# Attention and mixture of experts on one core: three sums put behind the next block's sixth product, and loads moved at the pass edges

## The chip, the cores and the metric

The kernel runs on 1 core of one Trainium2 chip. The metric is the device time of one execution in microseconds (us). Engines are named as in the profile: PE is TensorE, DVE is VectorE, ACT is ScalarE, POOL is GpSimd, SP is SyncE, which here issues all DMAs in one queue (SPq).

## What is computed

```python
def _attn_ref(q, k, v):                      # q, k, v: (4, 8, 576, 64)
    scores = scale * np.matmul(q, k.transpose(0, 1, 3, 2))
    mask = (rel >= 0) & (rel < 64)           # rel = query position - key position
    scores = np.where(mask, scores, -1e9)
    ...
    return np.matmul(softmax(scores), v)

def _moe_ref(x, w_gate, w1, w2):             # x: (2304, 512), E = 8, F = 1024
    P = np.exp(logits - logits.max())        # logits = x @ w_gate
    for _ in range(8):
        P /= P.sum(1, keepdims=True) + 1e-9
        P /= P.sum(0, keepdims=True) + 1e-9
        P *= N / E
    for e in range(E):
        out += P[:, e:e + 1] * (np.maximum(x @ w1[e], 0.0) @ w2[e])
```

All of it is float32. A matrix product is made of three products of rounded parts (high by high, high by low, low by high), so each operand is kept as a high part and a low part.

## The kernel before

The 2304 rows of x are 18 tiles of 128. A first stage computes attention and the gate (to about 207 us of the span). Then the experts run in three passes over six tiles each: pass 0 (to about 682 us), pass 1 (to about 1150 to 1182 us) and pass 2. The hidden columns of all experts form 30 groups of 256 columns; two groups make a unit, so there are 15 units (the first half of expert 0 was done in the first stage).

**First products (x by w1).** A group is computed as 2x2 blocks in Winograd's form: seven block products in the order 1, 5, 6, 2, 7, 3, 4 (`Group.product`, L212, six matmuls of 128x384 each) that add up in three PSUM tiles qa, qb, qc of two buffers each. ACT copies intermediate values (`b` from `a`, `p5`, `u2`), DVE makes the sums.

**Pass 0** (`Group.run`, then `mm2`): per unit two groups and then six ordinary second products (L271). While it runs, POOL and ACT split the weights into high and low parts, and these go to DRAM: w1 to `w1d`, and four sums of w2's blocks (`sums2`, four DVE operations per group, run one at a time by `sum_step`, L184) to `w2d`. The Sinkhorn iteration (`sk_col`, `sk_row`, L733 to L743) is spread over the second products of the first units by `step()`. `fetch2` loads raw w2 into one of four `stg` buffers.

**Passes 1 and 2.** Both products are in Winograd's form. `First(p, i)` (F_i below) is the first product of group i, `Second(p, u, o)` (S_u.o) one third of the second product of unit u; a number behind it is the block product, as in F2.4 or S0.0.7. The order of blocks is F0, F1, F2, S0.0, S0.1, S0.2, F3, F4, S1.0 and so on (`plan`), and within a block 6, 2, product 1 of the next block, 7, 3, product 5 of the next block, 4. The order is written out by hand: each engine runs its instructions in the order in which the code emits them. A `Second` product is six matmuls of 128x256 (L975); DVE adds its result to `acc` (`out_add`, L981), and the next product into the same PSUM tile waits for that.

After product 4 of a First block, DVE runs four operations in a row: sm0 (`relu_op`, L949) of qb, sm1 of c22 and sm0, sm3 of qc and sm1, and the low part `lo(1)` of qc (L900). POOL makes sm2 from sm1 and r22 (L954). The four results sm0 to sm3 are then split (`part_s`: ACT L903, POOL L904); the first at once, three by way of the list `urgent`. `bulk` is a list of w2 blocks to split (`split_w2`: ACT L882, POOL L883, then the next load `wr` by `load_w2`, L877, of three buffers). `do_bulk(1)` takes one entry, from `urgent` first.

**Pass edges.** Hooks behind given products load w1 of a later group (`load_w1`, L699, four DMAs into one of two `w1c` buffers, after product 4 of the group two before), store the finished rows (`out_rows`, L1031), reload the accumulator with the first stage's part for the new rows (`acc_rows`, L1035, six DMAs) and scale it (`scale0`, L1038, six DVE operations).

Of the kernel before, what the change touches and what calls it, by code (L numbers as in the profile page):

```python
# [11 lines left out]
ALU = mybir.AluOpType  # L12
# [9 lines left out]
def window_attention_sinkhorn_moe(ctx: ExitStack, tc: tile.TileContext, q, k, v, w_gate, w1, w2, out):  # L22
    nc = tc.nc
# [294 lines left out]
    with tc.manual_schedule():  # L318
# [383 lines left out]
        with ExitStack() as p2:  # L702
# [63 lines left out]
            for u in range(n_units):  # L766
                s = 2 * u
                last = u == n_units - 1

                def even(k):  # L770
                    if k == 0 and u > 0:
                        sum_step()
                        keep2(s + 2)
                    if k == 1:
                        if u:
                            split2(s + 2)
                            fetch1(s + 3)
                        keep1(s + 1 if u else 0)
                    elif k == 3:
                        if 4 <= u < 7:  # L780
                            next_sums(2, u - 4)
                        elif u == 7:
                            nc.sync.dma_start(out=xd_t[2], in_=side["xt"])
                        elif 9 <= u < 12:
                            next_sums(1, u - 9)

                def odd(k):
                    if k == 0 and u > 0:
                        sum_step()
                    if u == 0:  # L790
                        if k == 1:
                            split2(1)
                            fetch1(2)
                            keep1(1)
                    elif k == 0:
                        sums1(s + 2)
                    elif k == 1:
                        split2(s + 3)
                        fetch2(s + 4)
                        keep2(s + 3)  # L800

                Group(s).run(even)
                if last:
                    load_w1(0)
                Group(s + 1).run(odd)
                if last:
                    load_x(1, (0, 1, 2))
                    load_w1(1)
                if u == 0:
                    split2(2)  # L810
                    fetch1(3)
                    sums1(2)
                    split1(2)
                    split2(3)
                    fetch2(4)
                else:
                    split1(s + 2)
                sums1(s + 3)
                fetch2(s + 5)
                if last:  # L820
                    for k in (3, 4, 5, 6):
                        high_x(k)
                for t in range(TP):
                    if t == 0:
                        sums2(s + 4)
                        sums2(s + 5)
                    mm2(u, t)
                    sum_step(2 if last and t > 3 else 1)
                    if t % 2 == 0:
                        step()  # L830
                    if t == 2:
                        split1(s + 3)
                        fetch1(s + 4)
                    if t == 3 and not last:
                        keep1(s + 2)
                    if last:
                        low_x((3, 4, 5, 6, None, None)[t]) if t < 4 else None
                        if t == 4:
                            keep2(s + 4)
                if last:  # L840
                    keep2(s + 5)
# [3 lines left out]
        with ExitStack() as p3:  # L845
# [7 lines left out]

            HD = 2 * P
            W, R, G7 = {}, {}, {}
            bulk, urgent = [], []
            done_s = set()

            def do_bulk(n):
# [27 lines left out]
            def queue_w2(pu, ks):  # L887
                if pu:
                    bulk.extend([lambda k=k: split_w2(*pu, ORDER[k]) for k in ks])

            class First:
                def __init__(self, p, i):
                    self.p, self.i, self.G = p, i, Group(i)
# [13 lines left out]
                def step(self, n):  # L907
                    G = self.G
                    if n == 1:
                        self.a, self.b = ps["a"](), ps["b"]()  # L910
                        G.product(1, self.a, True)
                        nc.scalar.copy(out=self.b, in_=self.a)
                        do_bulk(1)
                    elif n == 5:
                        self.c, self.p5 = ps["c"](), new("p5", [P, NB], F32, 1)
                        G.product(5, self.c, True)
                        nc.scalar.copy(out=self.p5, in_=self.c)
                        do_bulk(1)
                    elif n == 6:
                        self.u2 = new("u2", [P, NB], F32, 1)  # L920
                        G.product(6, self.b, False)
                        nc.scalar.copy(out=self.u2, in_=self.b)  # L922
                        do_bulk(1)
                    elif n == 2:
                        self.g = new("G", [P, 7, 2, NB], F32R, 3)
                        G7[self.p, self.i] = self.g
                        self.r22 = new("r22", [P, NB], F32, 1)
                        G.product(2, self.a, False)
                        nc.scalar.activation(out=self.r22, in_=self.a, func=AF.Relu)
                        self.hi(2, self.a)  # L930
                    elif n == 7:
                        self.c22 = new("c22", [P, NB], F32, 1)
                        G.product(7, self.b, False)
                        G.add(self.c22, self.b, self.p5)
                        self.hi(0, self.c22)
                        self.lo(2, self.a)
                    elif n == 3:
                        G.product(3, self.c, False)
                        G.add(self.c, self.c, self.u2)
                        self.hi(1, self.c)  # L940
                        self.lo(0, self.c22)
                    else:
                        while urgent:
                            urgent.pop(0)()
                        G.product(4, self.b, False)
                        sm = self.sm = [new(f"sm{k}", [P, NB], F32, 1) for k in range(4)]

                        def relu_op(dst, src, other, op):
                            nc.vector.scalar_tensor_tensor(out=dst, in0=src, scalar=0.0, in1=other, op0=ALU.max, op1=op)  # L949

                        relu_op(sm[0], self.b, self.r22, ALU.add)
                        relu_op(sm[1], self.c22, sm[0], ALU.subtract)
                        relu_op(sm[3], self.c, sm[1], ALU.add)
                        nc.gpsimd.tensor_tensor(out=sm[2], in0=sm[1], in1=self.r22, op=ALU.add)  # L954
                        self.lo(1, self.c)
                        self.part_s(0)
                        urgent.extend([lambda k=k: self.part_s(k) for k in (1, 2, 3)])
                        wt1.pop(self.i)

            class Second:  # L960
                def __init__(self, p, u, o):
# [4 lines left out]
                def product(self, n, bank, start):  # L966
                    gp, wp = PROD[n]
                    p, u = self.p, self.u
                    while (p, u, wp) not in W or (p, 2 * u + 1, gp) not in done_s:
                        do_bulk(1)  # L970
                    cols = slice(self.o * P, (self.o + 1) * P)
                    j = 0
# [10 lines left out]
                def step(self, n):  # L983
# [10 lines left out]
                    elif n == 6:  # L994
                        self.product(6, self.b, False)
                        self.out_add(1, 1, self.b)
                    elif n == 2:
                        self.product(2, self.a, False)
                        self.out_add(1, 0, self.a)
# [47 lines left out]

            for _ in range(3):
                load_w2()
            queue_w2((1, 0), range(7))  # L1050
            out_rows(0, range(TP))
            first = plans[0][1][0]
            first.step(1)
# [2 lines left out]
            for p, F, S, flow in plans:  # L1056
# [5 lines left out]
                def hook(blk, step, *fs):  # L1062
                    hooks.setdefault((blk, step), []).extend(fs)

                hook(F[0], 6, lambda p=p: acc_rows(p))
                for i in range(n):
                    if i + 2 < n:
                        hook(F[i], 4, lambda i=i: load_w1(i + 2))
                    elif more:
                        hook(F[i], 4, lambda i=i: load_w1(i + 2 - n))  # L1070
                for t, (i, st) in enumerate(((1, 6), (1, 2), (1, 4), (2, 6), (2, 2), (2, 7))):
                    hook(F[i], st, lambda p=p, t=t: scale0(p, t))
                last = S[-1]
                if more:
                    hook(F[n - 1], 2, lambda p=p: new_x(p + 1))
# [11 lines left out]
                for k, blk in enumerate(flow):  # L1087
                    nx = flow[k + 1] if k + 1 < len(flow) else None
                    for st in (6, 2, -1, 7, 3, -5, 4):
                        if st > 0:  # L1090
                            go(blk, st)
                        elif nx:
                            go(nx, -st)
                a, b, c = last
                for blk, st in ((a, 1), (b, 1), (a, 2), (b, 2), (a, 5), (b, 5), (a, 6), (b, 6), (a, 7), (b, 7), (a, 3), (b, 3), (a, 4), (c, 1), (b, 4), (c, 5), (c, 6), (c, 2), (nextF, 1), (c, 7), (c, 3), (nextF, 5), (c, 4)):
                    if blk:
# [31 lines left out]
```

## Time and profile before

| | |
|---|---|
| median of 3 runs | 1646.04 us (1645.75 to 1646.67) |
| the profiled execution | 1643.92 us, span 1642.1 us, mean granted PE clock 0.992 |
| PE busy | 1580.5 us (96%), weight loads 1494.1 us |
| DVE, ACT, POOL busy | 912.2, 768.1, 973.8 us |
| chain that ended last | PE 84%, DVE 8% (3% at L949), DMA 4% |

The profile has a start time, a duration and the idle time before for each instruction. A row of the timeline reads: start in us, duration in us, engine, line, operation, output tile <- input tiles, shapes, how many instructions the row merges, and in square brackets the idle time of the engine just before and what ended it. Matmul ends are modelled with the pipeline's tail (a row of six matmuls lasts about 0.16 us longer than the distance to the next row), so idle time of PE is shown somewhat too small.

### The profile page before, as it was taken

The page shows a single profiled execution, that of the slowest core. Times are in us where ns is not written, and L with a number is a line of the kernel's source. Part 1 is how long each engine was busy: PE and PEld are TensorE (multiplying, and loading weights), DVE is VectorE, ACT ScalarE, POOL GpSimd, SP SyncE. Part 2 cuts the span into 40 slices and gives each one's busy share as a digit, 9 for nine tenths or more (in the row PEclk, how much of TensorE's full clock was granted, in tenths as well). Part 3 has the DMA queues.
Part 4 walks back from the last instruction along what each step waited for, and adds up shares of the span by engine and source line. Part 5 has one row for each costly group of instructions (what it writes and reads, how often), then busy time and mean ns, then how long its engine had stood idle before and what let it go on. Part 6 is the DMA issues. An engine that isn't in the chain of part 4 may idle for free.

```text
span 1642.1 us, 29136 instructions
## 1 busy us (share of the span) xinstructions
PE 1580.5 (96%) x10875; PEld 1494.1 (91%) x10875; DVE 912.2 (56%) x1754; ACT 768.1 (47%) x1676; POOL 973.8 (59%) x912
## 2 busy tenths in 40 slices
PE   8999989999999999979999999999899999999998
PEld 7888879989989989879999999999799999999998
DVE  6666456565555555454554554555565455455455
ACT  6566534433433433334544544544444454454452
POOL 5244466677776875165565565565566556556554
PEclk9999999999999999989999999999999999999999
DMA  9876476567667565854555555555855555555551
GB/s 223 193 162 151 140 247 240 205 225 273 233 236 256 212 237 212 291 211 165 184 184 171 183 186 172 182 187 170 309 181 185 171 184 185 172 182 186 172 181 65
DMA packets 206974, 324.50 MB, mean 198 GB/s; under 512 B 68528, under 2 KB 137136, under 8 KB 202864
## 3 DMA queue, kind: packets, MB, share of 16 engines
q1 hardware_dynamic: 206832, 322.64, 60.0%
q8 instruction: 85, 1.39, 0.3%
q14 instruction: 57, 0.47, 0.1%
HBM read 227.56 MB, written 88.08 MB: 192 GB/s over the span
## 4 chain that ended last, share of the span: by engine, by line
PE 84%; DVE 8%; DMA 4%; POOL 1%; ACT 1%; issue 1%; SPq 0%; DVEq 0%; POOLq 0%; ACTq 0%
PE qb L212 16%; PE yp L271 13%; PE qa L212 11%; PE qc L212 11%; PE qb L975 11%; PE qc L975 8%; PE qa L975 5%; DVE sm L949 3%; PE yp L556 3%; PE hp L542 3%; PE vp L462 1%; DMA stg<-in_moe_w_dram 1%; DVE G L900 1%; PE sp L412 1%; DMA wr<-w2d 1%
## 5 line engine op out<-in xcount | busy, mean ns | idle before, releaser
L883 POOL TENSOR_TENSOR wp<-wr,wp 128x512 fp32r<-128x512 f32 x210 | 270.3, 1305 | 178.5 <-ACT wp L882 174.5
L212 PE MATMUL qb<-xc,w1c 128*128 128x384 f32 x1620 | 323.0, 337 | 5.2 <-ACT u L922 4.8
L212 PEld LDWEIGHTS qb<-xc,w1c 128*128 128x128 f32 x1620 | 282.5, 189 | 6.2 <-ACT u L922 5.4
L904 POOL TENSOR_TENSOR G<-sm,G 128x384 fp32r<-128x384 f32 x240 | 241.1, 1032 | 47.8 <-ACT G L903 47.8
L975 PE MATMUL qb<-wp,G 128*128 128x256 f32 x1620 | 232.5, 286 | 24.8 <-DVE acc L981 24.8
L271 PE MATMUL yp<-w2c,g 128*128 128x512 f32 x1080 | 252.1, 392 | 0.6 <-DVE acc L290 0.6
L975 PEld LDWEIGHTS qb<-wp,G 128*128 128x128 f32 x1620 | 214.6, 191 | 30.9 <-DVE acc L981 30.7
L271 PEld LDWEIGHTS yp<-w2c,g 128*128 128x128 f32 x1080 | 202.9, 189 | 42.9 <-DVE acc L290 1.1
L212 PE MATMUL qa<-xc,w1c 128*128 128x384 f32 x1080 | 215.3, 339 | 10.6 <-DMA w1c<-w1d 10.6
L981 DVE SCALAR_TENSOR_TENSOR acc<-qb,prob,acc 128x256 f32<-128x256 f32 x270 | 130.3, 483 | 152.7 <-PE qb L975 152.5
L212 PE MATMUL qc<-xc,w1c 128*128 128x384 f32 x1080 | 214.4, 338 | 0.0
L212 PEld LDWEIGHTS qa<-xc,w1c 128*128 128x128 f32 x1080 | 190.6, 190 | 12.3 <-issue 11.1
L212 PEld LDWEIGHTS qc<-xc,w1c 128*128 128x128 f32 x1080 | 190.8, 190 | 0.0
L954 POOL TENSOR_TENSOR sm<-sm,r 128x384 f32<-128x384 f32 x60 | 61.1, 1018 | 184.4 <-DVE sm L949 156.2
L975 PE MATMUL qc<-wp,G 128*128 128x256 f32 x1080 | 150.2, 284 | 3.3 <-POOL wp L883 3.2
L903 ACT CAST G<-sm 128x384 fp32r<-128x384 f32 x240 | 120.6, 514 | 66.8 <-DVE sm L949 61.0
L173 POOL TENSOR_TENSOR w2c<-stg,w2c 128x512 fp32r<-128x512 f32 x60 | 83.6, 1415 | 112.1 <-PE qb L212 99.6
L975 PE MATMUL qa<-wp,G 128*128 128x256 f32 x1080 | 149.4, 283 | 0.5
L882 ACT CAST wp<-wr 128x512 fp32r<-128x512 f32 x210 | 124.6, 622 | 46.0 <-DMA wr<-in_moe_w_dram 36.6
L975 PEld LDWEIGHTS qc<-wp,G 128*128 128x128 f32 x1080 | 140.4, 193 | 3.7 <-POOL wp L883 3.4
L975 PEld LDWEIGHTS qa<-wp,G 128*128 128x128 f32 x1080 | 139.6, 191 | 1.3 <-DVE G L900 0.7
L225 DVE TENSOR_TENSOR c<-qb,p 128x384 f32<-128x384 f32 x60 | 33.4, 557 | 170.9 <-PE qb L212 169.0
(160 smaller groups left out, 2129.5 us busy)
## 6 DMA issues: line engine op xcount, KB each, us to landing
w1c<-w1d SPq DMA_DIRECT2D x180, 512.0 KB, 5.5
w1d<-w1c SPq DMA_DIRECT2D x30, 1792.0 KB, 7.0
stg<-in_moe_w_dram SPq DMA_DIRECT2D x66, 512.0 KB, 4.1
wr<-w2d SPq DMA_DIRECT2D x120, 256.0 KB, 3.1
wr<-in_moe_w_dram SPq DMA_DIRECT2D x90, 256.0 KB, 2.8
w2d<-tf SPq DMA_DIRECT2D x30, 512.0 KB, 3.6
w1c<-w1d SPq DMA_DIRECT2D x60, 256.0 KB, 2.8
xd_r<-xs SPq DMA_DIRECT2D x36, 128.0 KB, 2.7
```

What stands on the lines that cost most here:

```text
L173: nc.gpsimd.tensor_tensor(out=w[:, 1], in0=src[:, j], in1=f32(w[:, 0]), op=ALU.subtract)
L212: nc.tensor.matmul(bank, lhsT=w[:, ws, a, kk, :], rhs=xc[xs][:, b, kk, :], start=(first and j == 0), stop=(j == 5), skip_group_check=not f ...
L271: nc.tensor.matmul(yp, lhsT=g[:, a, o:o + P], rhs=w[:, x, :], start=(i == 0), stop=(i == 11))
L542: nc.tensor.matmul(hp, lhsT=w1s[c][:, a, kk, :], rhs=xs[j][:, b, kk, :], start=(i == 0), stop=(i == 3 * KD - 1))
L556: nc.tensor.matmul(yp, lhsT=g[:, a, o * P:(o + 1) * P], rhs=w[:, x, :], start=(i == 0), stop=(i == 11))
L882: nc.scalar.copy(out=t[:, :, 0, :], in_=r)
L883: nc.gpsimd.tensor_tensor(out=t[:, :, 1, :], in0=r, in1=f32(t[:, :, 0, :]), op=ALU.subtract)
L903: nc.scalar.copy(out=self.g[:, 3 + k, 0, :], in_=self.sm[k])
L904: nc.gpsimd.tensor_tensor(out=self.g[:, 3 + k, 1, :], in0=self.sm[k], in1=f32(self.g[:, 3 + k, 0, :]), op=ALU.subtract)
L954: nc.gpsimd.tensor_tensor(out=sm[2], in0=sm[1], in1=self.r22, op=ALU.add)
L975: nc.tensor.matmul(bank, lhsT=G7[p, 2 * u + g][:, gp, x, cols], rhs=W[p, u, wp][:, g, y, :], start=(start and j == 0), stop=(j == 5), skip ...
L981: nc.vector.scalar_tensor_tensor(out=at, in0=src, scalar=prob[:, FIRST[self.p] + t, self.e:self.e + 1], in1=at, op0=ALU.mult, op1=ALU.add)
```

## The change

Four things move; no operation is added or taken away.

1. In `First.step(4)` only sm0 and the split of sm0 are left. sm1, sm3, sm2, `lo(1)` and the entries for `urgent` go into a list `after`, which `late_sums()` runs in step 6 of the next block: behind the ACT copy in a First block, behind `out_add` in a Second block (and where the list is needed earlier, and after the last block of the flow).
2. In pass 0 the steps of `sums2` are dealt out otherwise: none behind the first two second products of unit 0, three in the even group and one in the odd group of a unit. The last two raw w2 groups are fetched about a unit earlier.
3. The w2 blocks of pass 1's first unit are put on the list `bulk` after F0.2 and not before F0.1; `do_bulk(1)` is also called after products 7 and 3 of the first three groups of pass 1.
4. The accumulator's reload goes from F0.6 to F1.6, its scaling from F1 and F2 to F2.3 (two operations) and products 2 and 3 of S0.0 and S0.1.

```diff
@@ pass 0
 def even(k):
+    if k != 1:
+        sum_step()
     if k == 0 and u > 0:
-        sum_step()
         keep2(s + 2)
     if k == 1:
...
+        if last:
+            fetch2(s + 5)
...
 def odd(k):
-    if k == 0 and u > 0:
+    if k == 0:
         sum_step()
...
-        fetch2(s + 4)
+        if not last:
+            fetch2(s + 4)
...
-fetch2(s + 5)
+if not last:
+    fetch2(s + 5)
...
     mm2(u, t)
-    sum_step(2 if last and t > 3 else 1)
+    if u or t > 1:
+        sum_step(2 if last and t > 3 else 1)
...
     if t == 2:
         split1(s + 3)
         fetch1(s + 4)
+        if u == n_units - 2:
+            fetch2(s + 6)
@@ passes 1 and 2
+def late_sums():
+    while after:
+        after.pop(0)()
...
     elif n == 6:                                     # First
         nc.scalar.copy(out=self.u2, in_=self.b)
+        late_sums()
         do_bulk(1)
...
     elif n == 7: ...                                 # First, and the same in n == 3
+        if self.p == 1 and self.i < 3:
+            do_bulk(1)
...
     relu_op(sm[0], self.b, self.r22, ALU.add)        # First, n == 4
-    relu_op(sm[1], self.c22, sm[0], ALU.subtract)
-    relu_op(sm[3], self.c, sm[1], ALU.add)
-    nc.gpsimd.tensor_tensor(out=sm[2], in0=sm[1], in1=self.r22, op=ALU.add)
-    self.lo(1, self.c)
     self.part_s(0)
-    urgent.extend([lambda k=k: self.part_s(k) for k in (1, 2, 3)])
     wt1.pop(self.i)
+
+    def rest():
+        relu_op(sm[1], self.c22, sm[0], ALU.subtract)
+        relu_op(sm[3], self.c, sm[1], ALU.add)
+        nc.gpsimd.tensor_tensor(out=sm[2], in0=sm[1], in1=self.r22, op=ALU.add)
+        self.lo(1, self.c)
+        urgent.extend([lambda k=k: self.part_s(k) for k in (1, 2, 3)])
+
+    after.append(rest)
...
     elif n == 6:                                     # Second
         self.product(6, self.b, False)
         self.out_add(1, 1, self.b)
+        late_sums()
...
-queue_w2((1, 0), range(7))
...
-hook(F[0], 6, lambda p=p: acc_rows(p))
+if p == 1:
+    hook(F[0], 2, lambda: queue_w2((1, 0), range(7)))
...
-for t, (i, st) in enumerate(((1, 6), (1, 2), (1, 4), (2, 6), (2, 2), (2, 7))):
-    hook(F[i], st, lambda p=p, t=t: scale0(p, t))
+hook(F[1], 6, lambda p=p: acc_rows(p))
+for t, (blk, st) in enumerate(((F[2], 3), (F[2], 3), (S[0][0], 2), (S[0][0], 3), (S[0][1], 2), (S[0][1], 3))):
+    hook(blk, st, lambda p=p, t=t: scale0(p, t))
```

PE's own order is the same in both kernels, row by row. DVE at the end of a unit's second First block (F8 of pass 1), which S3.0 follows; sm_9175 is sm0, 9176 sm1, 9178 sm3, G the low part, acc<-qb the result of product 6. Before:

```order
L981 SCALAR_TENSOR_TENSOR acc<-qc,prob,acc 128x256
L949 SCALAR_TENSOR_TENSOR sm_0_9175<-qb,r_0_9120 128x384
L949 SCALAR_TENSOR_TENSOR sm_0_9176<-c_0_9140,sm_0_9175 128x384
L949 SCALAR_TENSOR_TENSOR sm_0_9178<-qc,sm_0_9176 128x384
L900 SCALAR_TENSOR_TENSOR G_9119<-qc,G_9119 128x384
L981 SCALAR_TENSOR_TENSOR acc<-qb,prob,acc 128x256
L981 SCALAR_TENSOR_TENSOR acc<-qa,prob,acc 128x256
```

After:

```order
L1004 SCALAR_TENSOR_TENSOR acc<-qc,prob,acc 128x256
L966 SCALAR_TENSOR_TENSOR sm_0_9175<-qb,r_0_9120 128x384
L1004 SCALAR_TENSOR_TENSOR acc<-qb,prob,acc 128x256
L966 SCALAR_TENSOR_TENSOR sm_0_9176<-c_0_9140,sm_0_9175 128x384
L966 SCALAR_TENSOR_TENSOR sm_0_9178<-qc,sm_0_9176 128x384
L912 SCALAR_TENSOR_TENSOR G_9119<-qc,G_9119 128x384
L1004 SCALAR_TENSOR_TENSOR acc<-qa,prob,acc 128x256
```

The result of product 6 stands ahead of sm1, sm3 and the low part; where a First block follows, DVE's order is as it was.

SP's queue at the edge from pass 0 to pass 1 (wr are w2 blocks to split, w1c the weights of group 2, acc<-yd the reload). Before:

```order
L1031 DMA out_dram<-acc 128x512 x6
L877 DMA wr_7468<-in_moe_w_dram 128x2x256
L877 DMA wr_7482<-w2d_143 128x512
L877 DMA wr_7495<-in_moe_w_dram 128x2x256
L1035 DMA acc<-yd_101 128x512
...
L1035 DMA acc<-yd_106 128x512
L877 DMA wr_7525<-w2d_143 128x512
L877 DMA wr_7558<-in_moe_w_dram 128x2x256
L699 DMA w1c_7577<-w1d_115 128x512
L699 DMA w1c_7577<-w1d_115 128x1024 x3
```

After:

```order
L1055 DMA out_dram<-acc 128x512 x6
L885 DMA wr_7504<-in_moe_w_dram 128x2x256
L885 DMA wr_7519<-w2d_143 128x512
L885 DMA wr_7533<-in_moe_w_dram 128x2x256
L885 DMA wr_7547<-w2d_143 128x512
L699 DMA w1c_7562<-w1d_115 128x512
L699 DMA w1c_7562<-w1d_115 128x1024 x3
L1059 DMA acc<-yd_101 128x512
```

The weights of group 2 stand ahead of the six reloads and of one w2 block, still behind four w2 blocks. At the edge from pass 1 to pass 2 they stand ahead of the six reloads as well, with no w2 block between.

DVE behind the first second product of pass 0 (yp its result, tf<-stg a step of `sums2`, L741 to L735 a Sinkhorn step). Before:

```order
L278 TENSOR_TENSOR acc<-yp_3421,acc 128x512
L184 TENSOR_TENSOR tf_3419<-stg_3410 128x256
L741 TENSOR_REDUCE c<-qc 128x8
L742 RECIPROCAL c<-c 128x8
L743 TENSOR_TENSOR prob<-prob,c 128x18x8
L733 TENSOR_REDUCE r<-prob 128x18
```

After:

```order
L278 TENSOR_TENSOR acc<-yp_3421,acc 128x512
L741 TENSOR_REDUCE c<-qc 128x8
L742 RECIPROCAL c<-c 128x8
L743 TENSOR_TENSOR prob<-prob,c 128x18x8
L733 TENSOR_REDUCE r<-prob 128x18
```

The Sinkhorn step no longer stands behind the operation that reads the newly fetched w2.

## Rows read from the trace of the kernel before

**Rows 1.** Waits of PE: engine, line, waited-for, us in total, times, longest.

```profile
PE qb L975 <- DVE acc L981: 24.8, 29, 1.8
```

**Rows 2.** Timeline of pass 1 at the end of two units' First blocks.

```profile
791.42 0.98 PE L975 MATMUL qb<-wp,G 128*128 128x256 f32 x6 [0.75 <-DVE acc L981]
...
819.14 0.87 PE L975 MATMUL qb<-wp,G 128*128 128x256 f32 x6
819.40 0.56 DVE L949 SCALAR_TENSOR_TENSOR sm<-qb,r 128x384 f32<-128x384 f32 x1 [0.41 <-PE qb L212]
820.00 1.18 ACT L903 CAST G<-sm 128x384 fp32r<-128x384 f32 x2 [0.92 <-DVE sm L949]
820.07 0.56 DVE L949 SCALAR_TENSOR_TENSOR sm<-c,sm 128x384 f32<-128x384 f32 x1
...
821.20 0.55 DVE L900 SCALAR_TENSOR_TENSOR G<-qc,G 128x384 fp32r<-128x384 f32 x1
...
821.67 0.48 DVE L981 SCALAR_TENSOR_TENSOR acc<-qb,prob,acc 128x256 f32<-128x256 f32 x1
...
822.20 0.98 PE L975 MATMUL qb<-wp,G 128*128 128x256 f32 x6 [0.76 <-DVE acc L981]
```

**Rows 3.** Chain that ended last, same stretch: start, us, what.

```profile
811.61 2.10 PE qb L212 x12
...
823.18 1.44 PE qc L975 x12
```

**Rows 4.** Timeline of pass 0's first second products.

```profile
225.14 5.76 PE L271 MATMUL yp<-w2c,g 128*128 128x512 f32 x24
...
230.94 0.83 DVE L184 TENSOR_TENSOR tf<-stg 128x256 f32<-128x256 f32 x1 [5.09 <-DMA stg<-in_moe_w_dram]
...
235.48 0.94 PE L739 MATMUL qc<-prob,part 128*128 128x171 f32 x2 [4.58 <-DVE prob L735]
...
236.08 6.96 PE L271 MATMUL yp<-w2c,g 128*128 128x512 f32 x24
```

**Rows 5.** Timeline at the edge from pass 0 to pass 1.

```profile
682.00 1.23 PE L212 MATMUL qa<-xc,w1c 128*128 128x384 f32 x6
...
691.23 1.33 PE L212 MATMUL qb<-xc,w1c 128*128 128x384 f32 x6 [3.84 <-ACT u L922]
...
693.87 3.26 SPq L1035 DMA_DIRECT2D acc<-yd  x6
...
695.41 0.62 ACT L882 CAST wp<-wr 128x512 fp32r<-128x512 f32 x1 [2.56 <-DMA wr<-in_moe_w_dram]
...
700.51 21.04 SPq L699 DMA_DIRECT2D w1c<-w1d  x12
...
705.01 2.26 PE L212 MATMUL qa<-xc,w1c 128*128 128x384 f32 x6 [5.66 <-DMA w1c<-w1d]
...
733.50 1.67 PE L975 MATMUL qa<-wp,G 128*128 128x256 f32 x12
```

**Rows 6.** Windows: stretch, length, busy of PE, PEld, DVE, ACT, POOL; PEclk, DMA share, GB/s.

```profile
682.00:735.00 53.00, 38.16 (x199) 36.73 (x198) 24.18 (x44) 20.28 (x44) 27.36 (x24) 0.84 0.68 233
```

**Rows 7.** Timeline at the edge from pass 1 to pass 2.

```profile
1175.11 3.98 SPq L1035 DMA_DIRECT2D acc<-yd  x6
...
1176.10 2.27 PE L212 MATMUL qb<-xc,w1c 128*128 128x384 f32 x12
...
1184.31 2.26 PE L212 MATMUL qa<-xc,w1c 128*128 128x384 f32 x6 [4.91 <-DMA w1c<-w1d]
```

**Rows 8.** DMA issues: what, queue, kind, count, KB each, median us to landing.

```profile
w1c<-w1d SPq DMA_DIRECT2D x60, 256.0 KB, 2.8
```

**Rows 9.** Timeline, POOL and DVE at the same moment in pass 1's first group.

```profile
696.11 1.30 POOL L883 TENSOR_TENSOR wp<-wr,wp 128x512 fp32r<-128x512 f32 x1 [2.69 <-ACT wp L882]
...
696.49 1.33 DVE L900 SCALAR_TENSOR_TENSOR G<-c,G 128x384 fp32r<-128x384 f32 x1 [1.62 <-ACT G L896]
```

**Rows 10.** Lines by form: count | busy us, mean ns of one | idle before.

```profile
L949 DVE SCALAR_TENSOR_TENSOR sm<-qc,sm 128x384 f32<-128x384 f32 x60 | 33.5, 558 | 7.1
```

More of the change, by code (lines that the diff above doesn't have):

```diff
@@ L855, in window_attention_sinkhorn_moe @@
             W, R, G7 = {}, {}, {}
-            bulk, urgent = [], []
+            bulk, urgent, after = [], [], []
             done_s = set()
@@ L941, in step @@
                         self.lo(0, self.c22)
+                        if self.p == 1 and self.i < 3:
+                            do_bulk(1)
                     else:
@@ L969, in product @@
                     while (p, u, wp) not in W or (p, 2 * u + 1, gp) not in done_s:
+                        if not urgent and not bulk:
+                            late_sums()
                         do_bulk(1)
@@ L996, in step @@
                         self.out_add(1, 1, self.b)
+                        late_sums()
                     elif n == 2:
@@ L1093, in window_attention_sinkhorn_moe @@
                             go(nx, -st)
+                late_sums()
                 a, b, c = last
```

## Prediction

> **What bounds the kernel now.** I read the waits of PE first, because PE is busy nearly throughout and its order is unchanged: only its waits, and its rate, can give time back. The longest sum in that view is the wait of a Second product into qb for DVE's accumulation, 24.8 us in 29 places [rows 1]. The timeline shows what one is made of. At the end of a unit's First blocks, product 6 of the S block starts at 819.14 [rows 2]. Product 7 adds into the same qb, so it waits until DVE has added product 6 to the accumulator. DVE does that only behind sm0 (819.40), sm1 (820.07), sm3 and the low part (821.20): at 821.67, though product 6 had ended at 820.01. Product 7 starts at 822.20. Three products lie from 6 to 7 (6 itself, 2 and the next block's 1), each 0.72 (1.44 for two [rows 3]), so without the wait it would start at 819.14 + 2.16 = 821.30: 0.90 lost there, and a little more in refilling.
>
> The whole loss per unit is seen better from the period. Product 7 starts at 791.42 and at 822.20 [rows 2]: 30.78. A unit's work is 14 First products of 1.05 (2.10 for two [rows 3]) and 21 Second products of 0.72, 14.7 + 15.1 = 29.8 at most; with 1.045 it is 29.75. So 1.03 us per unit is lost. Of the 29 places, 26 are of this kind (13 in each of passes 1 and 2); the other three are the first unit of each pass and one in the last unit of pass 1, which other DVE work causes and which stays.
>
> The rest of PE's loss lies at the edges, read in the timelines there [rows 4, 5, 7]. In the window 682 to 735 the granted clock is 0.84 [rows 6], that is, a mixture of 1.2 and 2.4 GHz: behind the long waits six matmuls take 2.26 in place of about 1.2 [rows 5].
>
> **The change part by part.**
>
> *A, the late sums.* DVE now does sm0, then product 6's accumulation, then sm1, sm3 and the low part. sm0 ends at 819.96 and product 6 at 820.01, so the accumulation runs from about 820.05 to 820.53, well before 821.30: the wait goes. What is late next? sm1 can start at 820.45 (in DVE's pipe the operation behind an accumulation starts some 0.4 later), sm3 0.67 later (820.07 less 819.40) at 821.12, the low part at 821.6, ending at 822.15; then product 2's accumulation ends at 822.55 and product 7's at 823.05. The low part reads F's qc, whose buffer S.1's product 5 takes at 819.14 + 5 x 0.72 = 822.74: 0.6 to spare. Product 4 needs product 7's accumulation at 823.46: 0.4 to spare. POOL's sm2 and three splits come about 1 us later, but the S block in hand uses groups finished a unit before. Where a First block follows, DVE's order is unchanged, and ACT's r22 waits about 1 us longer for POOL, because the split of sm0 now stands ahead of sm2; the next product that needs ACT's later copy is over 2 us away. So A is worth 26 x 1.03 = 26.8. Its bounds are 27 and, if the wait only moves (rivals), 8 or nothing.
>
> *B, pass 0's first unit.* DVE's first `sums2` step waits 5.09 for its load, and the Sinkhorn step stands behind it, so PE waits 4.58 for prob [rows 4]. After that the 24 matmuls take 6.96 where the 24 before took 5.76: 1.2 more at the lower rate. With the step gone, the Sinkhorn step starts about 226 and PE reaches its matmul at 225.14 + 5.76 = 230.9; even at the length it has here (from 230.94 + 0.83 = 231.77 to 235.48, 3.7 us) it would be done at 229.7. Gain 4.58 + 1.2 = 5.8; between 3 (POOL's splitting of the next weights is reached sooner and holds PE) and 6.5. The steps moved into the even group cost nothing: pass 0 has no other wait for DVE worth naming.
>
> *C, the edge from pass 0 to pass 1.* From 682.00 to 733.50 [rows 5] PE runs 21 First and 10 Second products, 22.0 + 7.2 = 29.2 of work in 51.5: 22.3 lost. What of it stays? F0.7 no longer waits 3.84 for u2, since ACT's w2 splits, which wait for their loads, come later. PE then reaches F2.1 after 11 products, at 693.5, and waits for group 2's weights. These stand ahead of the reload now, but still behind a load that needs the fourth w2 split, whose own data came at 695.41 [rows 5]; with 0.62 on ACT, 1.3 on POOL [rows 9] and 0.3 to issue, the weights are issued about 697.8 (before 700.51). They land 2.8 later [rows 8] or, as here, 4.5 (705.01 less 700.51): 700.6 to 702.3, I take 701.2, because the reload no longer competes. So a wait of 7.7 stays. Behind it the lower rate stays, as after 705.01: 1.2 for the first product, twice that as an estimate, 2.3. The scaling, six DVE operations now among F2.3 and S0.0 to S0.1, makes the first S blocks late again, by 0 to 5; I take 4, since two operations stand ahead of sm0 and two more ahead of accumulations that PE waits for. C = 22.3 - 7.7 - 2.3 - 4 = 8.3, from 4 to 14.
>
> *D, the edge from pass 1 to pass 2.* Group 2's weights were issued behind the reload, at 1175.11 + 3.98 = 1179.1 [rows 7]. Their buffer is free when F0.4 ends, 1176.10 + 1.05 = 1177.15. Landing takes 2.8 [rows 8] to 5.2 (1184.31 less 1179.1): PE goes on between 1180.0 and 1182.4, I take 1181.2, 3.1 gained. A shorter wait leaves less of the lower rate, 0.9 as an estimate from the 1.05 that the product at 1184.31 lost; the first unit's wait of at most 1.8 [rows 1] shrinks by 0.5 net of the scaling. D = 4.5, from 1 to 6.
>
> Sum: 26.8 + 5.8 + 8.3 + 4.5 = 45.4. The profiled execution took 1643.9 (span 1642.1 and 1.8 around it), so it would take 1598.5; the median of the runs lies 2.1 above it, so 1600.6.
>
> **A rule that speaks against it.** sm1 reads two SBUF tiles, c22 and sm0. In pass 1's first group a DVE operation with two SBUF inputs, 0.55 long elsewhere [rows 2], took 1.33: it started at 696.49 inside a POOL operation that ran from 696.11 to 697.41, and ended 0.41 behind it [rows 9]. sm3, with one input in PSUM, is 558 ns on average [rows 10], whatever POOL does. So a late sm1 that meets the split of sm0 on POOL would be held. ACT's split of sm0 starts at 820.00 and takes about 0.5 [rows 2], so POOL starts at about 820.6; sm1 starts at about 820.45 and is ahead by some 0.15 us. That is close. The Trainium skill, "SBUF — State Buffer", section "Who interferes with whom", says the same: a VectorE instruction with two SBUF inputs and a GpSimd instruction that reads SBUF exclude each other, and whichever is first holds the other for its whole length. The trace agrees with that rule.
>
> **The rivals.**
>
> 1. *POOL is first* and holds sm1. It then ends at about 822.0 (820.6 + 1.0 + 0.4); sm3 and the low part end at 823.15. S.1's product 5, due at 822.74, waits 0.4 and product 4 0.1 more, with refilling 0.7: of 1.03 per unit 0.3 is left, A = 8. Time 1600.6 + 18.8 = 1619.4. For it speaks the narrow 0.15; against it the order of the two events. 13%.
> 2. *The wait moves whole.* DVE does the same work between F.4 and S.0's product 4; if its backlog is larger than I make it, product 4 or product 5 waits for as long as product 7 did: A = 0, 1627. Against it stands the slack of 0.4 and 0.6. 4%.
> 3. *Slower.* If POOL also held the operations with one SBUF input, all four late ones would wait about 1 us each behind its row of splits: the low part would end at 824.5, product 5 of S.1 wait 1.8 and refill, 2.0 per unit in place of 1.03. It turns the sum when more than 1.03 + 18.6 / 26 = 1.75 per unit is lost; at 2.0 the time is 1646.0 + 26 x 1.0 - 18.6 = 1653. Against it: 558 ns on average for sm3 [rows 10] with POOL busy more than half the time. 4%.
> 4. *It doesn't do what it says at the edges either:* A goes as in 2, and the weights are as late as before because the w2 blocks ahead of them are later; 1645. 3%.
>
> **How the numbers follow.** Forecast 1600.6 with 76%: its own range, from the bounds of B, C and D, is 1593 to 1611. To leave out no more than 2 in 10 the range reaches over rival 1: 1593 to 1621. A measurement of this kernel tells about 0.2% (3 us) from no change. Faster by more: forecast and rivals 1 and 2, 93%; within: rival 4, 3%; slower: rival 3, 4%.
>
> **What would show it.** A: the unit's period in passes 1 and 2 at 29.75 (rival 1: 30.5; rival 2: 30.8; rival 3: over 31.5), and PE's waits for the accumulation nearly gone; the order of sm1 and POOL's split of sm0 in the timeline decides rival 1. B: no PE wait at the second Sinkhorn matmul. C: no wait of F0.7, F2.1 at about 701 and not 705, and DVE's scaling in front of the waits in S0.0. D: F2.1 at about 2 us after PE gets there, not 4.9. I would be wrong above all if the period stays near 30.8, or if F2.1 of pass 1 comes later than 705 in the old clock.

## The result and the profile after

The changed kernel takes 1597.94 us (median of 4 runs, 1597.22 to 1599.11), the kernel before 1645.89 us (1644.12 to 1646.67) beside it: a ratio of 0.9711, 95% interval 0.9694 to 0.9728, 48 us less. The profiled execution took 1598.09 us, with a span of 1596.3 us, which is 45.8 us under the 1642.1 of before.

PE is busy for 1566.9 us of the span, 98% where it was 96%.

PE's waits in passes 1 and 2 of the changed kernel, against [rows 1]: engine, tile and line, waited-for, total us, times, longest.

```profile
PE qa L212 <- DMA w1c<-w1d: 9.3, 2, 8.5
PE qb L998 <- DVE acc L1004: 5.9, 5, 2.7
```

The wait for the accumulation went from 29 places and 24.8 us to 5 places and 5.9 us; none of the five lies in a steady unit. What is left lies at the edges.

Timeline of the changed kernel at the end of a unit's First blocks, the moment of [rows 2] (columns as there):

```profile
799.23 0.87 PE L998 MATMUL qa<-wp,G 128*128 128x256 f32 x6
...
803.78 0.87 PE L998 MATMUL qb<-wp,G 128*128 128x256 f32 x6
...
804.09 0.54 DVE L966 SCALAR_TENSOR_TENSOR sm<-qb,r 128x384 f32<-128x384 f32 x1
...
804.69 0.48 DVE L1004 SCALAR_TENSOR_TENSOR acc<-qb,prob,acc 128x256 f32<-128x256 f32 x1
805.09 0.55 DVE L966 SCALAR_TENSOR_TENSOR sm<-c,sm 128x384 f32<-128x384 f32 x1
805.26 1.26 POOL L916 TENSOR_TENSOR G<-sm,G 128x384 fp32r<-128x384 f32 x1 [0.44 <-ACT G L915]
...
805.92 0.88 PE L998 MATMUL qb<-wp,G 128*128 128x256 f32 x6
...
829.00 0.87 PE L998 MATMUL qa<-wp,G 128*128 128x256 f32 x6
```

Product 6 of the S block starts at 803.78. DVE adds it at 804.69, straight behind sm0, and product 7 starts at 805.92, 2.14 after product 6, with no wait. The same product a unit later (qa, 799.23 and 829.00) gives the period: 29.77, where it was 30.78.

Where the 45.8 us of span come from, each stretch from the same matmul to the same matmul in both traces (in us; a pair is the start and the end of a stretch, a single number its length):

| stretch | before | after | gain |
|---|---|---|---|
| pass 0, from its second products to pass 1 | 225.14 to 682.00 | 225.73 to 676.36 | 6.2 |
| edge 0 to 1, from F0.6 to S0.1's qa [rows 5] | 51.5 | 676.36 to 720.22: 43.9 | 7.6 |
| pass 1 from there to its last unit | 419.7 | 405.9 | 13.8 |
| edge 1 to 2, from the last unit to S0.1's qa | 52.9 | 46.4 | 6.5 |
| pass 2 from there to its last unit | 415.3 | 402.2 | 13.1 |
| first stage, and the last stores | | | -0.6 and -0.9 |

### The profile page after: what moved, and what is told of

Read it like the earlier page. It is cut to its first block, busy times and chain, and to the rows that moved or that the text cites. A ratio compares the mean times of both kernels' runs of the same rounds, so it can differ in the third digit from the quotient of the medians.

```text
span 1596.3 us, 29061 instructions
## 1 busy us (share of the span) xinstructions
PE 1566.9 (98%) x10875; PEld 1486.7 (93%) x10875; DVE 924.9 (58%) x1754; ACT 764.1 (48%) x1676; POOL 981.7 (61%) x912
## 3 DMA queue, kind: packets, MB, share of 16 engines
q8 instruction: 85, 1.39, 0.4%
## 4 chain that ended last, share of the span: by engine, by line
PE 91%; DVE 3%; DMA 2%; ACT 1%; POOL 1%; issue 1%; SPq 1%; DVEq 0%; POOLq 0%; ACTq 0%
PE qb L212 17%; PE yp L271 15%; PE qb L998 12%; PE qa L212 11%; PE qc L212 11%; PE qc L998 8%; PE qa L998 7%; PE yp L556 3%; PE hp L542 3%; PE vp L462 1%; PE tp L447 1%; PE sp L412 1%; PE tp L385 1%; DMA wr<-w2d 1%; POOL wp L891 0%
## 5 line engine op out<-in xcount | busy, mean ns | idle before, releaser
L916 POOL TENSOR_TENSOR G<-sm,G 128x384 fp32r<-128x384 f32 x240 | 250.0, 1053 | 218.1 <-ACT G L915 198.1
L998 PE MATMUL qb<-wp,G 128*128 128x256 f32 x1620 | 229.0, 283 | 5.9 <-DVE acc L1004 5.9
L1004 DVE SCALAR_TENSOR_TENSOR acc<-qc,prob,acc 128x256 f32<-128x256 f32 x180 | 86.6, 482 | 27.5 <-PE qc L998 26.9
```

Source lines behind the costliest of these rows:

```text
L916: nc.gpsimd.tensor_tensor(out=self.g[:, 3 + k, 1, :], in0=self.sm[k], in1=f32(self.g[:, 3 + k, 0, :]), op=ALU.subtract)
L998: nc.tensor.matmul(bank, lhsT=G7[p, 2 * u + g][:, gp, x, cols], rhs=W[p, u, wp][:, g, y, :], start=(start and j == 0), stop=(j == 5), skip ...
L1004: nc.vector.scalar_tensor_tensor(out=at, in0=src, scalar=prob[:, FIRST[self.p] + t, self.e:self.e + 1], in1=at, op0=ALU.mult, op1=ALU.add)
```

## The experiments

### Each part alone

The first kernel is the one before with nothing changed but the late sums; the second is the changed one with the sums put back behind sm0.

```diff
 # e1, against the kernel before
-    relu_op(sm[1], ...); relu_op(sm[3], ...); sm[2]; self.lo(1, self.c); urgent.extend(...)
+    after.append(rest)          # and late_sums() in step 6
 # e2, against the changed kernel
-    after.append(rest)
+    relu_op(sm[1], ...); relu_op(sm[3], ...); sm[2]; self.lo(1, self.c); urgent.extend(...)
```

> The kernel before with part 1 of the change alone (the late sums). Theory (the parts add, and the late sums give the period's 1.03 us per unit): period of passes 1 and 2 29.75 to 29.8 and not 30.78, 26 units, and about 0.5 us at the first unit of each pass: 1645.9 - 27.5 = 1618, within 2. Rival (the late sums pay only because the loads and the scaling were moved too, DVE being fuller at the edges): less than 20 us, 1626 or more.

> The changed kernel with the four operations back behind product 4 (parts 2 to 4 alone). Theory: the period is 30.78 again, and the edges and pass 0's first unit keep their gain of about 20: 1598 + 27 = 1625, within 2. Rival (interaction): above 1629, since the scaling that was moved into the first S blocks meets the sums there.

The late sums alone took 1615.46 us against 1643.42 (ratio 0.9831, 0.9816 to 0.9845): 28.0 less. The rest alone took 1624.90 (0.9886, 0.9868 to 0.9904): 18.5 less. Together 46.5, and the whole change gave 48: the parts add up within the intervals. The first time lies half a us under the range expected of it, but the kernel before took 2.5 less beside it than the 1645.89 that the range was worked out from; the gain of 28.0 is the expected 27.5. The traces say where each works. The edge from pass 1 to pass 2, group 2's First block, with the late sums alone and then with all but them:

```profile
1170.34 2.13 PE L212 MATMUL qa<-xc,w1c 128*128 128x384 f32 x6 [4.74 <-DMA w1c<-w1d]
```

```profile
1168.61 1.28 PE L212 MATMUL qa<-xc,w1c 128*128 128x384 f32 x6 [0.87 <-DMA w1c<-w1d]
```

The wait of F2.1 goes with the order of loads, whatever the sums do. And the wait for the accumulation goes with the sums, since in the second kernel it is as in [rows 1]:

```profile
PE qb L994 <- DVE acc L1000: 25.8, 29, 3.8
```

### Does POOL hold sm1, and when?

The prediction's first rival rests on 0.15 us: sm1 was to start that much before POOL's split of sm0. In the changed kernel it starts 0.17 before (805.09 and 805.26), so the order was as forecast. It is POOL that is held: 1.26 where the kernel's other splits take 1.02, ending 0.88 after sm1 does (806.52 and 805.64). To see the other order, a memset of a tile that nothing reads was put on DVE ahead of sm1; for the cost of the memset itself, the same one was put behind the low part.

```diff
 def rest():
+    pad = new("pad", [P, 512], F32, 1)      # ahead (256 columns, 512, or 512 and 256)
+    nc.vector.memset(pad, 0.0)
     relu_op(sm[1], self.c22, sm[0], ALU.subtract)
     ...
     self.lo(1, self.c)
+    nc.vector.memset(pad, 0.0)              # or here
     urgent.extend(...)
```

> The changed kernel with a memset of 128x256 on DVE just ahead of sm1 (a tile that nobody reads; some 0.2 to 0.4 us). Theory (whichever of sm1 and POOL's split of sm0 is first holds the other): sm1 now comes behind the start of POOL's operation, takes about 1.4 instead of 0.55, and product 5 or 4 of the next S blocks waits: period 30.2 to 30.5, time 1609 to 1617. Rival (no such hold; a delay of 0.4 fits into the slack of 0.4 to 0.6): period under 29.95, time under 1603.

> The same memset on DVE, but behind the late low part, so that sm1 keeps its place ahead of POOL. Both theories: DVE has as much more to do as in the kernel with the memset ahead of sm1, the slack of 0.4 for product 4 is used up, period 29.75 to 29.95, time 1598 to 1603. What the two differ by is the price of the hold.

1597.1 and 1598.5 us. The theory's 1609 to 1617 was missed: the memset took only 0.27, and although POOL's split is now recorded ahead of sm1, it is still POOL that is held:

```profile
804.55 0.27 DVE L974 MEMSET pad<- 128x256 f32 x1
...
804.62 1.49 POOL L916 TENSOR_TENSOR G<-sm,G 128x384 fp32r<-128x384 f32 x1 [0.43 <-ACT G L915]
...
804.74 0.49 DVE L966 SCALAR_TENSOR_TENSOR sm<-c,sm 128x384 f32<-128x384 f32 x1
```

> The changed kernel, and in each of the 30 late sums one more DVE operation, a memset of 128x512 of a tile that nothing reads, ahead of sm1. Beside it the same memset behind the low part. Theory (sm1, with two SBUF inputs, is held by POOL's split of sm0 when it comes second): the memset lasts about 0.4 to 0.55, sm1 comes to its place after POOL's split has started, lasts until that ends, 0.9 to 1.2 us in place of 0.55, and the units' period rises to 30.0 to 30.4: 1604 to 1615. Rival (no hold worth naming at this place): sm1 lasts 0.5 to 0.6, and this kernel takes the time of the other one within 2 us.

> The changed kernel, and in each of the 30 late sums one more DVE operation, a memset of 128x512 of a tile that nothing reads, behind the low part. It lengthens DVE's work as much as the same memset ahead of sm1 does, but leaves sm1 where it is. Theory: sm1 lasts 0.55 as before, the period stays at 29.8 to 29.95, and the time is 1598 to 1603. Rival (any 0.5 us more on DVE at this place is lost, whatever the order): 1604 to 1613, as with the memset ahead of sm1.

1603.47 and 1600.08 us: again no hold of sm1, though it starts 0.23 behind POOL's recorded start. The theory's time was missed by half a us and its mechanism altogether: sm1 is as short as the rival said, though the rival's 2 us between the two kernels are 3.4, in one run of each.

```profile
805.19 1.59 POOL L916 TENSOR_TENSOR G<-sm,G 128x384 fp32r<-128x384 f32 x1 [0.60 <-ACT G L915]
805.42 0.48 DVE L966 SCALAR_TENSOR_TENSOR sm<-c,sm 128x384 f32<-128x384 f32 x1
```

So the theory was changed: POOL takes hold of its input some 0.25 to 0.35 us after its recorded start. For it spoke, beside this run, two low parts with two SBUF inputs each: one started 0.38 behind POOL's recorded start and took 1.33 [rows 9], one in the changed kernel 0.36 behind it (802.70 and 802.34) and took 1.08. Two memsets together bring sm1 beyond that.

> The changed kernel, and in each of the 30 late sums two more DVE operations, memsets of 128x512 and 128x256 of a tile that nothing reads, ahead of sm1. In the run with the memset of 128x512 alone, sm1 started 0.23 us behind the recorded start of POOL's split of sm0, lasted 0.48, and POOL's split took 1.59: POOL was held, not sm1. Here sm1 starts about 0.25 later, 0.45 to 0.5 behind POOL's recorded start. Theory (whichever really reads first holds the other, and POOL reads some 0.25 to 0.35 behind its recorded start: there were DVE operations with two SBUF inputs that started 0.36 and 0.38 behind it and took 1.08 and 1.33): sm1 is held and lasts 0.9 to 1.0 on average in place of 0.49, POOL's split of sm0 takes 1.02 to 1.1, and the kernel takes 1612 to 1625. Rival (at this place DVE always holds POOL): sm1 lasts 0.5, POOL's split 1.8 to 1.9, and the time is 1604 to 1611.

> The changed kernel, and in each of the 30 late sums the same two memsets of 128x512 and 128x256 of a tile that nothing reads, behind the low part. sm1 lasts 0.55 as in the changed kernel; the memset of 128x512 alone cost 2 us in this place, so 1600 to 1606 by either theory. What the kernel with the memsets ahead of sm1 takes beyond this is the price of a late sm1; by the theory of a hold it is 10 to 20 us, by the rival 3 to 6.

1634.02 and 1610.13 us. The timeline of the first, end of a unit's First blocks:

```profile
809.81 0.48 DVE L974 MEMSET pad<- 128x512 f32 x1
...
809.99 1.02 POOL L916 TENSOR_TENSOR G<-sm,G 128x384 fp32r<-128x384 f32 x1 [0.61 <-ACT G L915]
...
810.42 0.27 DVE L975 MEMSET pad<- 128x256 f32 x1
810.60 0.82 DVE L966 SCALAR_TENSOR_TENSOR sm<-c,sm 128x384 f32<-128x384 f32 x1
...
812.61 0.98 PE L1001 MATMUL qc<-wp,G 128*128 128x256 f32 x6 [0.92 <-DVE G L912]
```

Now sm1 is the one that is held: it starts 0.61 behind POOL, lasts 0.82 and ends 0.41 after POOL's end (811.42 and 811.01), the same 0.41 as in [rows 9], while POOL's split takes its undisturbed 1.02. The memset itself does not keep POOL out: the first one starts 0.18 ahead of POOL's split, which is not longer for it. The low part comes late, and product 5 of S.1 waits for the qc that it reads, as the prediction's first rival had it. Of this wait of 0.92 the hold (0.82 less 0.49) is 0.33; the rest, by subtraction, comes of the memsets' own place ahead of the low part.

```profile
PE qc L1001 <- DVE G L912: 24.7, 27, 1.1
```

This run fits the changed theory, but the changed kernel's own trace speaks against it. There a low part starts only 0.05 behind POOL's split and is the one that is held:

```profile
702.46 1.02 POOL L916 TENSOR_TENSOR G<-sm,G 128x384 fp32r<-128x384 f32 x1 [1.55 <-ACT G L915]
702.51 1.38 DVE L912 SCALAR_TENSOR_TENSOR G<-c,G 128x384 fp32r<-128x384 f32 x1
```

The same is found once in each of four other runs, at 0.05 to 0.12 (1.31 to 1.39 long). So a delay of POOL alone does not explain who goes first: sm1 behind a memset does at 0.12 and 0.23, the low part behind a sum does not at 0.05. What tells them apart, the memset ahead or the operation itself, no run here shows.

| kernel | sm1 starts behind POOL's recorded start | sm1 | POOL's split | time |
|---|---|---|---|---|
| changed kernel | -0.17 | 0.55 | 1.26 | 1597.9 |
| 256 columns ahead | 0.12 | 0.49 | 1.49 | 1597.1 |
| 512 columns ahead | 0.23 | 0.48 | 1.59 | 1603.5 |
| 512 and 256 ahead | 0.61 | 0.82 | 1.02 | 1634.0 |
| 512 and 256 behind | -0.17 | 0.55 | 1.26 | 1610.1 |

Both times lie above what was expected of them. Behind the low part the memsets delay the accumulations, and that wait is 12.6 us in 31 places again, which the run with one memset did not show. Ahead of sm1 the memsets cost 23.9 more than behind: the hold (0.33 in each of 26 units) can be 8.6 of it, the place of the memsets the rest; these runs don't split the remaining 15 further.

### The waits that are left at the edges

In the changed kernel the edge from pass 0 to pass 1 reads:

```profile
676.36 1.23 PE L212 MATMUL qa<-xc,w1c 128*128 128x384 f32 x6
...
689.70 0.62 ACT L890 CAST wp<-wr 128x512 fp32r<-128x512 f32 x1 [3.29 <-DMA wr<-in_moe_w_dram]
...
691.69 0.32 SPq L885 DMA_DIRECT2D wr<-w2d  x1
...
692.11 1.81 SPq L699 DMA_DIRECT2D w1c<-w1d  x4
...
696.58 2.26 PE L212 MATMUL qa<-xc,w1c 128*128 128x384 f32 x6 [8.54 <-DMA w1c<-w1d]
...
711.69 2.64 DVE L1062 TENSOR_SCALAR acc<-acc,prob 128x512 f32<-128x512 f32 x2
...
715.63 0.98 PE L998 MATMUL qb<-wp,G 128*128 128x256 f32 x6 [2.73 <-DVE acc L1004]
...
718.72 1.67 PE L998 MATMUL qb<-wp,G 128*128 128x256 f32 x12 [0.48 <-DVE acc L1004]
...
720.22 1.60 PE L998 MATMUL qa<-wp,G 128*128 128x256 f32 x12
```

Two things stand out: SP holds back group 2's weights (692.11) until the fourth w2 split (ACT 689.70, then POOL) has made room for the load ahead of them (691.69), and two scalings (711.69) stand ahead of sm0 and of the accumulation that product 7 waits for. Each was changed alone.

```diff
 # e7, against the changed kernel: four of seven blocks behind the weights
-hook(F[0], 2, lambda: queue_w2((1, 0), range(7)))
+hook(F[0], 2, lambda: queue_w2((1, 0), range(3)))
 ...                                        # hook(F[0], 4): load_w1(2)
+hook(F[0], 4, lambda: queue_w2((1, 0), range(3, 7)))
 # e8, against the changed kernel: the first two scalings earlier and apart
-((F[2], 3), (F[2], 3), (S[0][0], 2), ...
+((F[2], 6), (F[2], 2), (S[0][0], 2), ...
```

> The changed kernel, with three of the seven w2 blocks of pass 1's first unit put on the list after F0.2 and the other four after F0.4, behind the loads of group 2's weights; so in SP's queue the weights stand behind three w2 loads and need the third split, not the fourth, before they can be issued. Theory (the wait of F2.1 in pass 1, 8.5 us, is the time until SP gets past the load that waits for a split): the weights are issued some 4 us earlier, the wait of F2.1 falls to about 4 to 5, the lower rate behind it partly goes, and the time is 1592 to 1596. Rival (the transfers of pass 0's end are the limit, and the weights land late wherever they stand): the wait stays at 8 or more, time 1597 to 1599. A further risk: the later blocks are split late and S0.0.3 or S0.0.4 waits 1 to 3 us.

> The changed kernel, with the first two of the six scalings behind F2.6 and F2.2 and not both behind F2.3. Theory (S0.0.7 of both passes waits because two scalings, 2.64 us together, stand ahead of sm0 and of product 6's accumulation on DVE): the waits of 2.73 and 0.48 us at pass 1's S0.0.7 and the next product shrink to under 1 together, the one of 0.56 in pass 2 goes, and the time is 1595 to 1597. Rival (DVE is late there for the sums of F2 themselves, or the scaling waits for the reload of the accumulator): the waits stay within 0.5, time 1597 to 1599.

The first: 1599.18 us, no gain. The mechanism was right, the weights were issued at 688.10 and the wait fell to 4.6, but the risk that was named came in full: from the place where the four blocks now stood the next split came at 698.24, the later ones slipped, and PE lost the gain again in the S blocks, at a lower rate behind it (eleven matmuls in 2.71, where twelve take 1.67 behind a short wait; the granted clock from 714 to 724 is 0.66).

```profile
691.94 2.26 PE L212 MATMUL qa<-xc,w1c 128*128 128x384 f32 x6 [4.61 <-DMA w1c<-w1d]
...
714.76 0.38 PE L998 MATMUL qb<-wp,G 128*128 128x256 f32 x1 [1.19 <-ACT wp L890]
717.78 2.71 PE L998 MATMUL qb<-wp,G 128*128 128x256 f32 x11 [2.63 <-POOL wp L891]
```

The second: 1594.06 us in one run. The wait of product 7 fell from 2.73 to 0.21, that of 0.48 stayed, and a new one of 0.74 appeared (product 5, for the low part):

```profile
712.89 0.98 PE L998 MATMUL qb<-wp,G 128*128 128x256 f32 x6 [0.21 <-DVE acc L1004]
...
715.32 0.98 PE L998 MATMUL qc<-wp,G 128*128 128x256 f32 x6 [0.74 <-DVE G L912]
...
716.78 1.66 PE L998 MATMUL qb<-wp,G 128*128 128x256 f32 x12 [0.48 <-DVE acc L1004]
...
718.27 1.60 PE L998 MATMUL qa<-wp,G 128*128 128x256 f32 x12
```

From F2.1 to S0.1's qa that is 1.6 us less in pass 1 (22.07 for 23.64) and 1.2 in pass 2. The time came out lower than the expected 1595 to 1597, by more than these 2.8, which one run can't tell from scatter.

The last kernel joins the two, with e7's fault mended: only the fourth split changes places with the weights' load, so that no later split slips.

```diff
-hook(F[0], 2, lambda: queue_w2((1, 0), range(7)))
+hook(F[0], 2, lambda: queue_w2((1, 0), range(3)))
 ...                                        # hook(F[0], 4): load_w1(2)
+hook(F[0], 4, lambda: split_w2(1, 0, ORDER[3]), lambda: queue_w2((1, 0), range(4, 7)))
 ...                                        # and e8's scaling
```

> The changed kernel with two edits at the edges. First, the split of the fourth w2 block of pass 1 goes from the place ahead of F0.4 to the place behind the load of group 2's weights, so that the weights stand behind three w2 loads in SP's queue and no split is later than before by more than F0.4's own; the run that put off all four last blocks had a wait of F2.1 of 4.6 us, but lost 3.8 us to late splits (POOL 2.6, ACT 1.2) and the lower rate behind them. Second, the scaling behind F2.6 and F2.2, as in the run that gained 3.5 us. Theory: both gains add, the wait of F2.1 is 4.5 to 5, no wait for a split, 1588.5 to 1592. Rival (the split is late here too, because ACT reaches it only behind F1): PE waits 2 us or more for wp in the first S blocks, 1593 to 1596.

1591.10 us (median of 4, 1589.17 to 1592.17) against 1644.31: ratio 0.9675, 0.9659 to 0.9691, which lies below the interval of the changed kernel (0.9694 to 0.9728), some 6 us less. This version beats both. Its edge:

```profile
675.99 1.23 PE L212 MATMUL qa<-xc,w1c 128*128 128x384 f32 x6
...
687.51 2.15 SPq L699 DMA_DIRECT2D w1c<-w1d  x4
...
689.69 0.62 ACT L890 CAST wp<-wr 128x512 fp32r<-128x512 f32 x1 [2.96 <-DMA wr<-in_moe_w_dram]
...
692.66 2.26 PE L212 MATMUL qa<-xc,w1c 128*128 128x384 f32 x6 [4.99 <-DMA w1c<-w1d]
...
714.27 1.60 PE L998 MATMUL qa<-wp,G 128*128 128x256 f32 x12
```

The fourth split runs at the same moment as before (689.69), but the weights are issued 4.6 earlier (687.51 for 692.11; counted from F0.6, 4.2) and no product waits for a w2 block. From F0.6 to S0.1's qa it takes 38.28, 5.6 less than the changed kernel's 43.86. What remains of the wait, 4.99, is the third split ahead of them and a landing of 5.2.

## Why the prediction was right, point by point

**A, the late sums: right in mechanism and size.** Forecast 26.8 from a period of 29.75; measured 29.77, and 13.8 and 13.1 in the two passes, 26.9. Alone it gave 28.0. Two small effects were not in it: the late sums removed the wait for u2 at the last edge (0.92 in the trace of before, 0.17 now, 1.16 in the kernel with all but the late sums), and made one wait in the last unit of pass 1 longer, where DVE also works on the next pass's x: 1.68 in the changed kernel and 1.69 with the late sums alone, 0.92 with all but them.

```profile
1130.79 1.70 PE L998 MATMUL qb<-wp,G 128*128 128x256 f32 x12 [1.68 <-DVE acc L1004]
...
1145.78 1.32 PE L212 MATMUL qb<-xc,w1c 128*128 128x384 f32 x6 [0.17 <-ACT u L934]
...
1153.12 1.29 PE L212 MATMUL qa<-xc,w1c 128*128 128x384 f32 x6 [0.79 <-DMA w1c<-w1d]
...
1167.95 0.98 PE L998 MATMUL qb<-wp,G 128*128 128x256 f32 x6 [0.56 <-DVE acc L1004]
1170.95 1.69 PE L998 MATMUL qb<-wp,G 128*128 128x256 f32 x12 [0.43 <-DVE acc L1004]
```

**B, pass 0's first unit: right.** Forecast 5.8, measured 6.2. PE reaches the Sinkhorn matmul without a wait and goes on at full rate, where [rows 4] show 4.58 of wait and 6.96 for the same 24:

```profile
225.73 5.76 PE L271 MATMUL yp<-w2c,g 128*128 128x512 f32 x24
231.33 0.45 PE L739 MATMUL qc<-prob,part 128*128 128x171 f32 x2
231.50 5.76 PE L271 MATMUL yp<-w2c,g 128*128 128x512 f32 x24
```

**C, the edge from pass 0 to pass 1: right, slightly too large.** Forecast 8.3, measured 7.6. F0.7 no longer waits for u2. The weights were issued 15.75 after F0.6 started (692.11 less 676.36), the forecast's 697.8 less 682.00 is 15.8 (its own terms add up to 697.6); but they landed after 4.47, the upper of the two values that stood there, and a value near the middle had been taken. So PE, whose 11 products end at about 687.9, stands still for 8.7 and not 7.7. Behind it the clock is lower, 0.73 in the window from 696.58 to 705.01, and seven First products take 9.47 where 7.35 would do: 2.1, the forecast had 2.3. The scaling left waits of 2.73 and 0.48; with the refilling behind them seven Second products take 8.91 (711.31 to 720.22) where 5.04 would do, 3.9, and the forecast had 4. So the landing cost 1.0 more than forecast, and the two other terms gave 0.3 of it back.

```profile
696.58:705.01 8.43, 8.43 (x36) 8.43 (x37) 3.57 (x6) 3.92 (x9) 3.32 (x4) 0.73 0.86 330
```

(A window of the changed kernel: stretch, length, busy of PE, PEld, DVE, ACT, POOL, granted clock, DMA share, GB/s, as in [rows 6].)

**D, the edge from pass 1 to pass 2: right in mechanism, mis-sized.** Forecast 4.5 with a bound of 6, measured 6.5. The step that failed is the landing of the weights: between 2.8 and 5.2 the prediction took a value that put F2.1 at 1181.2, 4.05 after the buffer comes free. They were issued at 1150.28 and F2.1 started at 1153.12, 2.84 later, at the lower end. So the wait fell by 4.1 (4.91 to 0.79) and not by 3.1. The lower rate behind the wait went altogether: the seven First products from F2.1 on take 7.42 (granted clock 1.00) where they took 8.95 (0.81), 1.5 for an estimate of 0.9. The estimate went by the first product alone, and in the trace of before the second was slow too, 1.63 from 1186.37 to 1188.00. The first unit's wait fell from 1.8 to 0.56 and 0.43 in two pieces; with the refilling, the way from there to S0.1's qa is 11.9 for 12.8, 0.9 for 0.5. The u2 wait (0.75 less) and the longer one of the last unit (0.76 more) cancel. Before, and then after:

```profile
1186.37 1.79 PE L212 MATMUL qb<-xc,w1c 128*128 128x384 f32 x6
1188.00 2.27 PE L212 MATMUL qc<-xc,w1c 128*128 128x384 f32 x12
...
1193.26 0.87 PE L975 MATMUL qa<-wp,G 128*128 128x256 f32 x6
```

```profile
1160.54 0.87 PE L998 MATMUL qa<-wp,G 128*128 128x256 f32 x6
```

**The sum: closer than its terms, by luck.** 45.4 was forecast for the span, and 45.8 measured. But B and D gave 0.4 and 2.0 more than forecast and C 0.7 less, while the first stage and the last stores lost 1.5 that the sum did not have. The median was put 2.1 above the profiled execution, as it was for the kernel before; here it lies 0.2 below it (1597.94 and 1598.09), and most of the 2.7 between 1600.6 and the measured median comes from that.

**The rivals.** The first was refuted by the order at 805.09 and 805.26. What it names does exist: with both memsets ahead sm1 was held at 0.61 behind POOL's recorded start, and product 5 waited. How wide the margin of sm1 is without a memset no run shows; with one it went first even 0.23 behind, but a low part was held at 0.05. The second (the wait moves whole) fell with the period. The third (operations with one SBUF input held too) has no support: in all these runs sm3 is 557 or 558 ns on average, as in [rows 10], and so long even where sm1 is held. The fourth fell with both edges.

The Trainium skill, "SBUF — State Buffer", "Who interferes with whom", says that the ports which VectorE and GpSimd share are an exclusive lock and that issue order decides who blocks. The run with both memsets agrees (sm1 held until 0.41 after POOL's end), but in the runs with one memset the POOL instruction is recorded first, by 0.12 and 0.23, and yet is the one that is held (1.49 and 1.59 long). The measurement decides: the order of recorded starts can't be taken for the order that counts.

## What to carry to other kernels

An operation that frees a buffer for the next product should stand in its engine's queue ahead of all that merely has to be done some time; the price of the wait is read from the unit's period and not from the single wait, and what is late next is found by adding up the moved operations one by one. At the edges one load behind a stalled one costs as much as the stall: look what the issuing queue is waiting for, and move that one step behind the urgent load, not the whole list. A wait that goes can also give back the lower rate behind it: here 1.2 us of 6.2 at pass 0's first unit (granted clock 0.81 from 236.08 to 242.90 before, 1.00 from 231.50 to 237.20 now) and 1.5 of 6.5 at the last edge (0.81 and 1.00).

## What was not expected of the hardware

When POOL and a DVE operation with two SBUF inputs meet, the order of their recorded starts does not tell which is held. Behind a memset, sm1 went first although recorded 0.12 and 0.23 us after POOL's split. A low part was held although recorded only 0.05 after it (1.38 long, 0.55 undisturbed), and others at 0.36 (1.08) and 0.38 (1.33 [rows 9]); sm1 was held at 0.61 (0.82). Why is open. The lengths are steady: a held DVE operation ends 0.4 after POOL's end, and when POOL is the one that is held, it ends 0.88 after DVE's operation does, in three kernels alike (806.52 and 805.64, 806.11 and 805.23, 806.78 and 805.90).
